# Entry of a fused adaLN transformer block: c turned on the tensor engine, modulation weights by tile, q and k side by side, high parts by ScalarE

## The chip, the cores and the metric

One core of a Trainium2 chip runs the whole program. The metric is the device time of one execution in microseconds (us). The engines are named as in the profile: PE is the tensor engine (PEld its weight loads), DVE the vector engine, ACT the scalar engine (ScalarE), POOL GpSimd, SP the queue that issues most transfers. Each engine works through its own instructions in order and waits on semaphores for the others.

## What is computed

The block is adaptive layer norm, attention with 32 heads, and a gated feed-forward part, on 2048 rows of 576 values. Only the front of it matters here:

```
mod = (silu(c) @ w_mod)            # c: 1 x 576, w_mod: 576 x 3456, six vectors of 576
h   = layernorm(x) * (1 + ca) + sa # x: 2048 x 576; sa, ca are the first two of the six
q, k, v = h @ wqkv                 # then softmax attention, projection, feed-forward
```

Products are made in 32-bit accuracy: an operand is split into a rounded "high" part (type fp32r) and a "low" part, the rest, and three products (high x high, high x low, low x high) are added up in PSUM.

## The kernel before

**Constants of c.** `craw` (128 x 5) takes c with its 576 values spread over the partitions (L403, L404), ACT makes the sigmoid (L405) and loads the table of the exponential ahead (L407), DVE multiplies (L408) and spreads the result over 32 columns each into `mrow` (L424), where `modulate` takes it as PE's weights.

**Modulation.** `load_mod` loads the first third of w_mod, 576 x 1152, into `wm`: two transfers of two row tiles of 128 and one of the last 64 rows (L124, L125). `modulate` (L149) multiplies them into one PSUM bank: for row tiles 0 to 4 a 384- and a 192-column product for each of two vectors, then, once more over all five tiles, the 64 columns that are left. DVE copies the result to `row`, PE transposes it (L190), and DVE writes the two vectors as columns `mcol` (L200, L201).

**Rows.** x comes in four chunks of 512 rows (4 tiles each, `rows_in`). `normalized` makes statistics on DVE (L207, L208), the inverse root with one power on POOL (L221) and eight small DVE steps, and scales the four x tiles (L232). PE transposes them with an identity matrix (`ident`, L241). `ln_transpose` (L244) then works in five steps over the 576 features: ACT applies `mcol` and writes `full` in fp32 (L251), DVE rounds it to the high part in `hT` (L259) and subtracts for the low part (L260); the fifth step is half as high and has its high and low part both on DVE (L264 to L266).

**Queries, keys, values.** `project_qk` takes one weight tile for q and one for k through 14 products of 512 columns each (L336) into one PSUM bank each; ACT takes the high part (L342), DVE the low part (L343), and SP stores both. `project_v` does the same for 288 columns of v (L389, L394) into `vaug`, which POOL fills with ones first (L458). `splits` and `split_v` make the high part of the weights on ACT (L277) and the low part on DVE (L278).

**Order.** In this entry the three engines PE, DVE and ACT run exactly in the order in which the code is written (a manual schedule); a scheduler places POOL and SP work. Chunk by chunk the code reads: q/k products, v products, transposes and modulation of the next chunk, statistics of the chunk after it. After the entry a second stage makes the other q/k tiles (the list `tiles`) while scores of the first heads are already multiplied for their maxima: `project_qk` there calls `run`, which issues four score products (L550) after each accumulation; DVE reduces each (L556). Seven PSUM banks go round in the order of allocation for all of these, so which score waits for which earlier bank follows from that order. Here the scheduler sets the order.

Of the kernel before, what the change touches and what calls it, by code (L numbers as in the profile page):

```python
# [15 lines left out]
F32 = mybir.dt.float32  # L16
# [7 lines left out]
P = 128  # L24
S = 2048
D = 576
# [59 lines left out]
def tile_block(ctx, tc, x_in, wqkv, wo, w_gate, w_up, w_down, c_in, w_mod, out):  # L86
# [62 lines left out]
    def modulate(row, wm, pieces, takes, between=()):  # L149
# [8 lines left out]
        pm = bank()  # L158
        for parts in pieces:
            for t in range(last + 1):  # L160
                if between and t == 2 and parts is pieces[0]:
                    between[0]()
                k = ksize(t)
                for v in range(2):
                    for g, to, f0, n in parts:
                        q = 32 * (2 * v + g)
                        nc.tensor.matmul(
                            pm[q : q + 32, to : to + n], sc_b[:k, t, :],
                            wm[t][:k, v * D + f0 : v * D + f0 + n],
                            start=t == 0, stop=t == last, tile_position=(0, q),  # L170
                        )
        if between:
            between[1]()
        if pieces is HALVES:
# [12 lines left out]
        if between:  # L187
            between[2]()
        for b in range(3):
            nc.tensor.transpose(pt[:, b * P : (b + 1) * P], row[:, b * P : (b + 1) * P], ident)  # L190
        cols = pt[:, 0:384].rearrange("p (b q) -> p b q", q=P)
        for v, (dst, add) in enumerate(takes):
# [51 lines left out]
    def ln_transpose(pool, zs, dst, c0, turned=()):  # L244

        cols = slice(c0, c0 + 512)
        for i in range(5):
# [79 lines left out]

    def project_qk(both, ahead=None):

        pl = stages[0].tile([P, 2, 1024], F32R, name="pl")  # L330
        for i, ((parts, wh, wl), ch) in enumerate(both):
            acc = bank()
            cols = slice(ch * 512, (ch + 1) * 512)
            ts_ = terms(wh, wl, slice(0, P))
            for n, (w, t) in enumerate(ts_):
                nc.tensor.matmul(  # L336
                    acc, w, hT[:, t, cols], start=n == 0, stop=n == len(ts_) - 1
                )
            if ahead:
# [60 lines left out]
    with tc.tile_pool(name="ln", bufs=2) as ln:  # L400
        craw = early.tile([P, 5], F32, name="craw")
        nc.vector.memset(craw, 0.0)
# [3 lines left out]
        warm = early.tile([P, 1], F32, name="warm")  # L406
        nc.scalar.activation(warm, sc[:, 0:1], AF.Exp)  # L407
        nc.vector.tensor_mul(sc, sc, craw)  # L408

        def rows_in(ch):  # L410
# [7 lines left out]
        def normalized(xs, first=None):  # L418
            mv = ln.tile([P, 4, 2], F32, name="mv")
            rs = ln.tile([P, 4], F32, name="rs")  # L420
            for j, xt in enumerate(xs):
                ln_stats(ln, xt[:, :D], mv[:, j, :])
            if first is not None:
                nc.vector.tensor_copy(  # L424
                    first[:, 384:544].rearrange("p (t c) -> p t c", c=32), sc.unsqueeze(2).to_broadcast([P, 5, 32])
                )
# [10 lines left out]
        wvp = wv0.enter_context(tc.tile_pool(name="wv0", bufs=1))  # L437
        with tc.tile_pool(name="wmp", bufs=1, side="right") as wmp:
            rows_now = rows_in(0)
            wm = wmp.tile([P, 5, 2 * D], F32, name="wm")  # L440
            wm = load_mod(wm[:, 0:4, :], wm[:, 4, :], 0)
            row = wmp.tile([P, 544], F32, name="mrow")
            zs = normalized(rows_now, row)
# [8 lines left out]
            for _ in modulate(  # L452
                row, wm, QUARTERS, [(mcol[:, 1, :], 0.0), (mcol[:, 0, :], 1.0)],
                (turn_some(0, 1, 2), turn_some(3), turn_some(4)),
            ):
                pass
        stages.append(right.enter_context(tc.tile_pool(name="stage", bufs=2, side="right")))
        nc.gpsimd.memset(vaug, 1.0)  # L458
        splits[0]()
        ln_transpose(ln, None, hT, 0, turned)  # L460
        splits[1]()
        split_v()
        with tc.tile_pool(name="kdp", bufs=1) as kdp:
            zs = normalized(rows_now)
            pls = []
            for ch in range(NCH):
                pls.append(project_qk([(wt, ch) for wt in wts]))
                project_v(wv, 0, 4 * ch)
# [1370 lines left out]
```

## Time and profile before

| what | value |
|---|---|
| median of 3 runs (lowest, highest) | 2770.05 us (2768.8, 2773.7) |
| the profiled execution, its own time | 2771.59 us |
| its span in the profile | 2769.8 us |
| PE busy, share of the span | 99% |
| DVE busy | 83% |
| ACT busy | 57% |
| POOL busy | 30% |
| granted TensorE clock, mean | 0.999 of full |

The span is what the profile covers; the execution's own time lies 1.8 us above it. The page divides the span into 40 slices of 69 us, and PE is busy 90% or more in all but the first (70%). So the entry is the stage where PE has most of its idle time, and the rows further down are taken from the first 80 us, and from the stage of the score maxima around 145 us.

### The profile page before, as it was taken

The numbers are of one execution on the slowest core, as the hardware profiler recorded it, in microseconds if no ns is written. First come the engines' busy times: TensorE is split into PE (matmuls) and PEld (weight loads), VectorE is DVE, ScalarE is ACT, GpSimd is POOL, SyncE is SP. The second block draws the span as 40 slices with busy tenths as digits, with TensorE's granted clock in tenths as the row PEclk, the third lists the DMA queues.
The fourth block names the chain that finished last, engine by engine and source line by source line (L and its number), as shares of the span: only waits on it lengthen the run. The fifth ranks groups of instructions, "written<-read, shape, count | busy, mean of one in ns | idle before, by whom it ended". The sixth has DMA issues, their size and how long they took to land.

```text
span 2769.8 us, 50752 instructions
## 1 busy us (share of the span) xinstructions
PE 2735.4 (99%) x18429; PEld 1829.0 (66%) x18429; DVE 2291.4 (83%) x4333; ACT 1590.3 (57%) x3020; POOL 838.6 (30%) x1061
## 2 busy tenths in 40 slices
PE   7999999999999999999999999999999999999999
PEld 5975444444444544444444888888888888888888
DVE  7278989999999889999883888888888677777777
ACT  3215999999999789999987323333333122222221
POOL 3122237888853214660133222222221100000000
PEclk9999999999999999999999999999999999999999
DMA  5342344555553121332246766767768965656653
GB/s 175 122 153 98 89 106 170 189 189 188 185 174 104 51 64 55 137 98 74 64 115 240 250 225 230 243 221 268 278 239 295 330 203 195 203 196 201 199 198 117
DMA packets 185378, 480.03 MB, mean 173 GB/s; under 512 B 30304, under 2 KB 94308, under 8 KB 175016
## 3 DMA queue, kind: packets, MB, share of 16 engines
q1 hardware_dynamic: 164216, 377.39, 41.0%
q0 software_dynamic: 20912, 99.41, 10.0%
q8 instruction: 145, 2.38, 0.4%
q14 instruction: 105, 0.86, 0.1%
HBM read 294.80 MB, written 181.38 MB: 172 GB/s over the span
## 4 chain that ended last, share of the span: by engine, by line
PE 92%; DVE 3%; DMA 2%; POOL 1%; issue 1%; SPq 0%; ACT 0%; DVEq 0%; ACTq 0%; POOLq 0%
PE x L1226 27%; PE o L655 19%; PE s L1070 12%; PE s L550 10%; PE d L1376 8%; PE d L1308 6%; PE s L336 4%; PE s L799 2%; PE s L389 1%; DMA big<-in_w_mod_dram 1%; POOL big L141 0%; PE d L1574 0%; DVE Oa L1380 0%; DVE w L1216 0%; DMA raw<-in_B_w_up_dram 0%
## 5 line engine op out<-in xcount | busy, mean ns | idle before, releaser
L1074 ACT ACTIVATE p<-s 128x512 f32<-128x512 f32 x2048 | 1069.9, 626 | 85.4 <-PE s L1070 60.2
L556 DVE TENSOR_REDUCE mx<-s 128x1 f32<-128x512 f32 x1568 | 1001.3, 684 | 102.8 <-PE s L550 72.1
L655 PE MATMUL o<-p,vaug 128*32 128x256 f32 (+1 forms) x5848 | 594.8, 477 | 2.0 <-ACT oT L673 2.0
L550 PE MATMUL s<-k,q 54*128 54x512 f32 x1920 | 550.2, 436 | 0.0
L1070 PE MATMUL s<-q,k 56*128 56x512 f32 x1920 | 530.8, 439 | 1.3 <-DMA q<-mrows 1.3
L1070 PEld LDWEIGHTS s<-q,k 56*128 56x128 f32 x1920 | 251.8, 185 | 252.8 <-DVE mx L556 74.2
L550 PEld LDWEIGHTS s<-k,q 54*128 54x128 f32 x1920 | 277.8, 185 | 210.6 <-DVE mx L561 65.3
L1226 PE MATMUL x<-k,w 128*128 128x512 f32 x1512 | 368.1, 391 | 0.0
L1226 PEld LDWEIGHTS x<-k,w 128*128 128x128 f32 x1512 | 277.3, 188 | 53.4 <-issue 1.7
L655 PEld LDWEIGHTS o<-p,vaug 128*32 128x32 f32 x5848 | 117.1, 108 | 205.6 <-issue 188.0
L1226 PE MATMUL x<-big,w 128*128 128x512 f32 x1008 | 246.1, 393 | 4.9 <-DVE u L1740 4.9
L1376 PE MATMUL d<-wd,hh 128*128 128x288 f32 x1248 | 249.6, 295 | 0.9 <-DMA wd<-wds 0.5
L1226 PE MATMUL x<-w,w 128*128 128x512 f32 x1008 | 244.6, 391 | 0.0
L1226 PEld LDWEIGHTS x<-big,w 128*128 128x128 f32 x1008 | 186.6, 189 | 41.0 <-DVE u L1740 5.3
L1226 PEld LDWEIGHTS x<-w,w 128*128 128x128 f32 x1008 | 184.5, 188 | 33.9
L1376 PEld LDWEIGHTS d<-wd,hh 128*128 128x128 f32 x1248 | 202.3, 188 | 4.4 <-DMA wd<-wds 0.9
L1376 PE MATMUL d<-wd,hl 128*128 128x288 f32 x624 | 184.5, 296 | 0.0
L1380 DVE TENSOR_TENSOR Oa<-Oa,d 128x288 f32<-128x288 f32 x312 | 136.7, 453 | 54.9 <-PE d L1376 50.9
L561 DVE CUSTOM_DVE_ANT_0 over<-s,over 128x512 f32<-128x512 f32 x240 | 163.8, 682 | 0.9
L559 ACT ACTIVATE over<-s 128x512 f32<-128x512 f32 x240 | 147.9, 616 | 3.0 <-PE s L550 1.0
L1235 ACT ACTIVATE sg<-x 128x512 f32<-128x512 f32 x36 | 21.5, 598 | 206.8 <-PE x L1226 206.7
L1207 ACT CAST w<-S 128x768 fp32r<-128x768 f32 x71 | 59.4, 836 | 137.3 <-POOL S L1180 135.4
(265 smaller groups left out, 3820.4 us busy)
## 6 DMA issues: line engine op xcount, KB each, us to landing
ws<-w SPq DMA_DIRECT2D x126, 640.0 KB
w<-ws SPq DMA_DIRECT2D x126, 640.0 KB
wd<-wds SPq DMA_DIRECT2D x19, 1152.0 KB
k<-kd SPq DMA_DIRECT2D x60, 360.0 KB
wds<-w POOLq DMA_DIRECT2D x18, 1152.0 KB, 5.2
wtd<-t POOLq DMA_DIRECT2D x32, 576.0 KB, 4.8
wt<-wtd SPq DMA_DIRECT2D x64, 288.0 KB
wd<-wds SPq DMA_DIRECT2D x52, 288.0 KB
```

Of the source, the lines that this page charges most:

```text
L336: nc.tensor.matmul(acc, w, hT[:, t, cols], start=n == 0, stop=n == len(ts_) - 1)
L550: nc.tensor.matmul(sp, qs[rows, qt * P : (qt + 1) * P], ks[rows, at * 512 : (at + 1) * 512], start=True, stop=True,)
L556: nc.vector.tensor_reduce(to, sp, axis=AX.X, op=ALU.max)
L559: nc.scalar.activation(over, sp, AF.Relu)
L561: nc.vector.tensor_tensor_reduce(out=over, in0=sp, in1=over, scale=1.0, scalar=LOWEST, op0=ALU.add, op1=ALU.max, accum_out=mx[:, h * n + q ...
L655: nc.tensor.matmul(acc[32 * j : 32 * j + 32, cols], vaug[:, kt, (2 * p + h) * VW : (2 * p + h) * VW + 32], probs[2 * c + h][:, cols], star ...
L1070: nc.tensor.matmul(sT, ks[rows, kcols], qs[rows, c * 512 : (c + 1) * 512], start=True, stop=True)
L1074: state["exp"] = nc.scalar.activation(pr, sT, AF.Exp, scale=SCALE)
L1226: nc.tensor.matmul(acc[v], w[:, v, a, :], X[s][:, b, :], start=first and n == 0, stop=n == 6, skip_group_check=not first,)
L1308: nc.tensor.matmul(acc, a[:, rows], w[:, k, :], start=n == 0, stop=n == 2)
L1376: nc.tensor.matmul(acc[:, :HALF], a[:, f, rows], w[:, f, cols], start=n == 0, stop=n == 5)
L1380: nc.vector.tensor_add(Oa[:, t, cols], Oa[:, t, cols], acc[:, :HALF])
```

## The change

c is loaded as five rows of 128 on ACT's queue into the scratch tile `row`, multiplied by its sigmoid there, and turned to columns by one PE transpose, placed between the third and the fourth x tile's statistics. `load_mod` has one transfer for each row tile when it is called for the first third. `modulate` goes over the row tiles once and puts the last 64 columns into a second PSUM tile of the pool `po`; the transposes of x that stood among its products now stand behind them. `ln_transpose` has ACT write the high part too, straight from PSUM, in place of DVE's rounding. `project_qk` allocates both banks at its start, and for chunk 0 alternates between q and k in groups of three products. Both weight splits stand ahead of chunk 0's modulation. POOL's fill of `vaug` becomes 17 small ones that write only the columns of ones.

```
     def load_mod(a, b, i):
         cols = slice(2 * D * i, 2 * D * (i + 1))
+        if not i:
+            for t in range(5):
+                k = ksize(t)
+                nc.sync.dma_start((a[:, t, :] if t < 4 else b)[:k], w_mod[t * P : t * P + k, cols])
+            return [a[:, t, :] for t in range(4)] + [b]
...
         pm = bank()
-        for parts in pieces:
-            for t in range(last + 1):
-                if between and t == 2 and parts is pieces[0]:
-                    between[0]()
+        pms = [pm] if pieces is HALVES else [pm, po.tile([P, 512], F32, name="o")]
+        for t in range(last + 1):
+            for to_, parts in zip(pms, pieces):
...
-            nc.vector.tensor_copy(row[:, 0:256], pm[:, 0:256])
+            nc.vector.tensor_copy(row[:, 0:192], pm[:, 0:192])
             for q in (0, 64):
-                nc.vector.tensor_copy(row[q : q + 32, 256:384], pm[q : q + 32, 256:384])
+                nc.vector.tensor_copy(row[q : q + 32, 192:384], pm[q : q + 32, 192:384])
+                q += 32
+                nc.vector.tensor_copy(row[q : q + 32, 192:256], pms[1][q : q + 32, 192:256])
...
             if i < 4:
                 modulated(full, 0, P)
-                nc.vector.tensor_copy(dst[:, i, cols], full)
+                modulated(dst[:, i, cols], 0, P)
                 nc.vector.tensor_sub(dst[:, 4 + i, cols], full, dst[:, i, cols].bitcast(F32))
...
-    def project_qk(both, ahead=None):
+    def project_qk(both, ahead=None, together=False):
+        accs = [bank() for _ in both]
+        all_ = [terms(wh, wl, slice(0, P)) for (_, wh, wl), _ in both]
+        places = [(i, n) for i in range(len(both)) for n in range(len(all_[i]))]
+        if together:
+            places.sort(key=lambda at: min(at[1] // 3, 4))
+        for i, n in places:
...
-        nc.sync.dma_start(craw[:, 0:4], c_in[0, 0:DM].rearrange("(t p) -> p t", p=P))
-        nc.sync.dma_start(craw[0:64, 4:5], c_in[0, DM:D].rearrange("(p o) -> p o", o=1))
-        nc.scalar.activation(sc, craw, AF.Sigmoid)
...
+                if first is not None and j == 3:
+                    turned_c = po.tile([P, 512], F32, name="o")[:, 0:5]
+                    nc.vector.tensor_mul(first[0:5, 256:384], first[0:5, 0:P], first[0:5, P:256])
+                    nc.tensor.transpose(turned_c, first[0:5, 256:384], ident[0:5, 0:5])
...
+            nc.scalar.dma_start(row[0:4, 0:P], c_in[0, 0:DM].rearrange("(t p) -> t p", p=P))
+            nc.scalar.dma_start(row[4:5, 0:64], c_in[0:1, DM:D])
...
-        nc.gpsimd.memset(vaug, 1.0)
-        splits[0]()
+        ones = vaug[:, :, 0 : H * VW].rearrange("p t (h e) -> p t h e", e=VW)
+        for t in range(NT):
+            nc.gpsimd.memset(ones[:, t, :, DH:VW], 1.0)
+        nc.gpsimd.memset(vaug[:, :, H * VW :], 1.0)
+        for split in splits:
+            split()
         ln_transpose(ln, None, hT, 0, turned)
-        splits[1]()
         split_v()
```

What that does to the order on the engines is seen at three places. On SP, the first place is the head of the program, here before and then with the change:

```order
L414 DMA x<-in_A_x_dram 128x576
L403 DMA craw<-in_c_dram 128x4x1
L404 DMA craw<-in_c_dram 64x1
L414 DMA x<-in_A_x_dram 128x576 x3
L124 DMA wm<-in_w_mod_dram 128x2x1152 x2
L125 DMA wm<-in_w_mod_dram 64x1152
L270 DMA wq_raw<-in_A_wqkv_dram 128x4x128
```

```order
L417 DMA x<-in_A_x_dram 128x576 x4
L125 DMA wm<-in_w_mod_dram 128x1152 x4
L125 DMA wm<-in_w_mod_dram 64x1152
L276 DMA wq_raw<-in_A_wqkv_dram 128x4x128
L280 DMA wq_raw<-in_A_wqkv_dram 64x128 x2
```

The two transfers of c are gone from between the first and the second x tile, and w_mod comes in five pieces in place of three.

On ACT, the second place is chunk 0, from the weights' high part on, before and then with the change (`full` and `hT` are what the modulation writes, `s_...` the transposed x in PSUM):

```order
L277 CAST wq_h<-wq_raw 128x640
L251 ACTIVATE full<-s_234,mcol 128x512
L251 ACTIVATE full<-s_239,mcol 128x512
L251 ACTIVATE full<-s_244,mcol 128x512
L251 ACTIVATE full<-s_271,mcol 128x512
L251 ACTIVATE full<-s_281,mcol 128x512
L277 CAST wq_h<-wq_raw 128x640
L277 CAST wv_h<-wv_raw 128x1440
```

```order
L283 CAST wq_h<-wq_raw 128x640 x2
L257 ACTIVATE full<-s_261,mcol 128x512
L257 ACTIVATE hT<-s_261,mcol 128x512
L257 ACTIVATE full<-s_266,mcol 128x512
L257 ACTIVATE hT<-s_266,mcol 128x512
L257 ACTIVATE full<-s_271,mcol 128x512
L257 ACTIVATE hT<-s_271,mcol 128x512
L257 ACTIVATE full<-s_286,mcol 128x512
L257 ACTIVATE hT<-s_286,mcol 128x512
L257 ACTIVATE full<-s_291,mcol 128x512
L283 CAST wv_h<-wv_raw 128x1440
```

Each chunk has nine activations in place of five, and both weight casts now stand ahead of the first. The other three chunks read alike.

On PE, the third place is the stage of the score maxima, with bank numbers (`s5_1441` is a tile in bank 5; `hT` products are a q/k accumulation, `t1,q0` products are scores), with the change only; before, four scores always stood together behind an accumulation:

```order
L344 MATMUL s5_1441<-hT_123,wq_l_1436 128x512
L567 MATMUL s3_1484<-t1_1058,q0_1050 128x512
L567 MATMUL s4_1487<-t1_1058,q0_1050 128x512
L567 MATMUL s6_1493<-t1_1058,q0_1050 128x512
L344 MATMUL s0_1510<-hT_123,wq_h_1435 128x512 x2
L344 MATMUL s0_1510<-hT_123,wq_l_1436 128x512
L567 MATMUL s5_1490<-t1_1058,q0_1050 128x512
L344 MATMUL s0_1510<-hT_123,wq_l_1436 128x512
L344 MATMUL s0_1510<-hT_123,wq_h_1435 128x512
```

With both banks taken at the start of `project_qk`, the third score of the second group falls on the bank that the accumulation just finished (5). The scheduler has put it behind the first 11 products of the next accumulation (the pair of rows above it stands for a run of 11), and DVE's low part of that bank ahead of its fourth reduction. This occurs 11 times. Further on, the engines' orders are the same as before, but for one exchange of two loads on SP ahead of this stage.

## Rows read from the trace of the kernel before

**Rows 1.** Page: busy time, share of the span, instructions of each engine.

```profile
PE 2735.4 (99%) x18429; PEld 1829.0 (66%) x18429; DVE 2291.4 (83%) x4333; ACT 1590.3 (57%) x3020; POOL 838.6 (30%) x1061
```

**Rows 2.** PE's waits, 0 to 110 us: total us, times, longest.

```profile
PE s L167 <- DMA wm<-in_w_mod_dram: 12.2, 1, 12.2
```

**Rows 3.** Timeline to 24 us: start, us, engine, line, operation [idle before, releaser].

```profile
1.19 0.42 SPq L403 DMA_DIRECT2D craw<-in_c_dram  x1
...
2.29 1.52 SPq L414 DMA_DIRECT2D x<-in_A_x_dram  x3
...
8.73 0.27 DVE L424 COPY mrow<-sc 128x160 f32<-128x160 f32 x1
...
17.86 0.16 PEld L167 LDWEIGHTS s<-wm,mrow 64*32 64x32 f32 x8 [0.62 <-DMA wm<-in_w_mod_dram]
...
18.97 0.73 ACT L277 CAST wq_h<-wq_raw 128x640 fp32r<-128x640 f32 x1 [10.74 <-DMA wq_raw<-in_A_wqkv_dram]
...
19.55 0.42 DVE L182 COPY mrow<-s 128x256 f32<-128x256 f32 x1 [5.09 <-PE s L167]
...
21.29 2.85 ACT L251 ACTIVATE full<-s,mcol 128x512 f32<-128x512 f32 x4 [1.59 <-DVE mcol L201]
```

**Rows 4.** Stretches: span, length, PE busy (count), clock, DMA share, GB/s.

```profile
1.50:4.00 2.50, 0.00 (x0) 1.00 0.66 135
4.00:13.00 9.00, 0.77 (x10) 1.00 0.97 349
```

**Rows 5.** Timeline of chunks 0 and 1, 22 to 47 us.

```profile
22.56 0.69 DVE L260 TENSOR_TENSOR hT<-full,hT 128x512 fp32r<-128x512 f32 x1
...
23.17 0.42 DVE L259 CAST hT<-full 128x512 fp32r<-128x512 f32 x1
...
28.70 1.65 DVE L278 TENSOR_TENSOR wv_l<-wv_raw,wv_h 128x1440 fp32r<-128x1440 f32 x1
...
30.27 0.81 DVE L207 BATCH_NORM_STATS2 st<-x 128x6 f32<-128x288 f32 x2
...
37.03 2.05 DVE L232 TENSOR_SCALAR x<-x,mv,rs 128x576 f32<-128x576 f32 x4
...
39.21 2.65 PE L241 MATMUL s<-ident,x 128*128 128x128 f32 x20
...
39.91 2.86 ACT L251 ACTIVATE full<-s,mcol 128x512 f32<-128x512 f32 x4
...
46.59 0.82 DVE L207 BATCH_NORM_STATS2 st<-x 128x6 f32<-128x288 f32 x2
```

**Rows 6.** Timeline of chunk 2 and the start of chunk 3, 56 to 77 us.

```profile
56.96 2.12 ACT L251 ACTIVATE full<-s,mcol 128x512 f32<-128x512 f32 x3 [2.30 <-PE s L241]
...
57.76 1.29 POOL L364 TENSOR_TENSOR kd_e<-pl 128x512 f32<-128x512 f32 x1 [0.91 <-DVE pl L343]
57.77 1.55 DVE L259 CAST hT<-full 128x512 fp32r<-128x512 f32 x1
...
59.36 1.67 DVE L260 TENSOR_TENSOR hT<-full,hT 128x512 fp32r<-128x512 f32 x1
...
67.13 0.82 DVE L207 BATCH_NORM_STATS2 st<-x 128x6 f32<-128x288 f32 x2
...
76.11 2.08 PE L241 MATMUL s<-ident,x 128*128 128x128 f32 x17 [0.17 <-DVE x L232]
```

**Rows 7.** A stretch behind it, PE: span, length, PE busy (count), clock, DMA share, GB/s.

```profile
90.00:110.00 20.00, 20.00 (x113) 1.00 0.68 213
```

**Rows 8.** Timeline in the stage of the score maxima, one period.

```profile
145.41 0.73 PE L550 MATMUL s<-t,q 54*128 54x512 f32 x4
145.94 2.48 DVE L556 TENSOR_REDUCE mx<-s 128x1 f32<-128x512 f32 x4 [0.98 <-PE s L550]
...
148.34 0.68 DVE L343 TENSOR_TENSOR pl<-s,pl 128x512 fp32r<-128x512 f32 x1
149.47 0.73 PE L550 MATMUL s<-t,q 54*128 54x512 f32 x4
```

More of the change, by code (lines that the diff above doesn't have):

```diff
@@ L172, in modulate @@
         if between:
-            between[1]()
+            between[0]()
         if pieces is HALVES:
@@ L181, in modulate @@
             nc.vector.memset(row[:, 256:384], 0.0)
-            nc.vector.tensor_copy(row[:, 0:256], pm[:, 0:256])
+            nc.vector.tensor_copy(row[:, 0:192], pm[:, 0:192])
             for q in (0, 64):
-                nc.vector.tensor_copy(row[q : q + 32, 256:384], pm[q : q + 32, 256:384])
+                nc.vector.tensor_copy(row[q : q + 32, 192:384], pm[q : q + 32, 192:384])
+                q += 32
+                nc.vector.tensor_copy(row[q : q + 32, 192:256], pms[1][q : q + 32, 192:256])
         yield
         pt = bank()
-        if between:
-            between[2]()
         for b in range(3):
             nc.tensor.transpose(pt[:, b * P : (b + 1) * P], row[:, b * P : (b + 1) * P], ident)
+        if between:
+            between[1]()
         cols = pt[:, 0:384].rearrange("p (b q) -> p b q", q=P)
@@ L326, in load_qk @@
         return parts, wh, wl
-    def project_qk(both, ahead=None):
+    def project_qk(both, ahead=None, together=False):
         pl = stages[0].tile([P, 2, 1024], F32R, name="pl")
[L331 to L338, printed above, removed]
+        accs = [bank() for _ in both]
[4 more added lines that the diff above has]
+        for i, n in places:
+            (w, t), ch = all_[i][n], both[i][1]
+            nc.tensor.matmul(
+                accs[i], w, hT[:, t, ch * 512 : (ch + 1) * 512],
+                start=n == 0, stop=n == len(all_[i]) - 1, skip_group_check=together,
+            )
+            if n < len(all_[i]) - 1:
+                continue
+            acc = accs[i]
             if ahead:
@@ L400, in tile_block @@
     with tc.tile_pool(name="ln", bufs=2) as ln:
-        craw = early.tile([P, 5], F32, name="craw")
-        nc.vector.memset(craw, 0.0)
-        nc.sync.dma_start(craw[:, 0:4], c_in[0, 0:DM].rearrange("(t p) -> p t", p=P))
-        nc.sync.dma_start(craw[0:64, 4:5], c_in[0, DM:D].rearrange("(p o) -> p o", o=1))
-        nc.scalar.activation(sc, craw, AF.Sigmoid)
-        warm = early.tile([P, 1], F32, name="warm")
-        nc.scalar.activation(warm, sc[:, 0:1], AF.Exp)
-        nc.vector.tensor_mul(sc, sc, craw)
         def rows_in(ch):
@@ L421, in normalized @@
             for j, xt in enumerate(xs):
+                if first is not None and j == 3:
+                    turned_c = po.tile([P, 512], F32, name="o")[:, 0:5]
+                    nc.vector.tensor_mul(first[0:5, 256:384], first[0:5, 0:P], first[0:5, P:256])
+                    nc.tensor.transpose(turned_c, first[0:5, 256:384], ident[0:5, 0:5])
                 ln_stats(ln, xt[:, :D], mv[:, j, :])
             if first is not None:
+                nc.vector.tensor_copy(sc, turned_c)
                 nc.vector.tensor_copy(
@@ L438, in tile_block @@
         with tc.tile_pool(name="wmp", bufs=1, side="right") as wmp:
+            row = wmp.tile([P, 544], F32, name="mrow")
+            nc.vector.memset(row[0:5, 0:P], 0.0)
+            nc.scalar.dma_start(row[0:4, 0:P], c_in[0, 0:DM].rearrange("(t p) -> t p", p=P))
+            nc.scalar.dma_start(row[4:5, 0:64], c_in[0:1, DM:D])
             rows_now = rows_in(0)
+            nc.scalar.activation(row[0:5, P:256], row[0:5, 0:P], AF.Sigmoid)
+            warm = early.tile([P, 1], F32, name="warm")
+            nc.scalar.activation(warm[0:5], row[0:5, P : P + 1], AF.Exp)
             wm = wmp.tile([P, 5, 2 * D], F32, name="wm")
             wm = load_mod(wm[:, 0:4, :], wm[:, 4, :], 0)
-            row = wmp.tile([P, 544], F32, name="mrow")
             zs = normalized(rows_now, row)
@@ L453, in tile_block @@
                 row, wm, QUARTERS, [(mcol[:, 1, :], 0.0), (mcol[:, 0, :], 1.0)],
-                (turn_some(0, 1, 2), turn_some(3), turn_some(4)),
+                (turn_some(0, 1, 2), turn_some(3, 4)),
             ):
@@ L466, in tile_block @@
             for ch in range(NCH):
-                pls.append(project_qk([(wt, ch) for wt in wts]))
+                pls.append(project_qk([(wt, ch) for wt in wts], together=not ch))
                 project_v(wv, 0, 4 * ch)
```

2 lines of the change are left out of this document (1 added, 1 removed).

## Prediction

> **What bounds the kernel now.** I read the page first: PE is busy for 99% of the span [rows 1], so a gain can only come from where PE stands still. PE's waits say where: the largest is one wait of 12.2 us for the first modulation weights, at the start [rows 2]. Then I followed the first 80 us in the timeline to see how long the entry holds PE back. From the transposes of chunk 3, which start at 76.11, PE no longer pauses: 20.00 us busy of 20 from 90 to 110 [rows 6, 7]. Everything behind that keeps its order on every engine but for the maxima stage, so a us won or lost before 76.11 arrives at the end, and one won on an engine that PE doesn't wait for is lost.
>
> The 76 us fall into two parts. Up to 21.29, when ACT modulates the first tile, transfers set the time: the last weight tile lands at 17.86 (W), PE, DVE copies and PE's transposes of the two vectors follow, and ACT starts 3.43 later (F) [rows 3]. From there to 76.11 the path is on DVE: PE takes the low parts as they come, and the next chunk's statistics stand behind them in DVE's order (at 30.27, 46.59, 67.13), their scaling ahead of the next transposes [rows 5, 6].
>
> **Transfers (the first term).** Before, c's two transfers stand between the first x tile and the rest: the issue of c starts at 1.19 and that of the next x tile at 2.29, so 1.10 us of SP [rows 3]. c also comes as 576 single values, and from 1.5 to 4 the engines move 135 GB/s at a share of 0.66, against 349 GB/s at 0.97 from 4 to 13 [rows 4]. Had the first stretch run at the second's rate, 2.5 x 214 GB/s = 0.54 MB more would have been moved, worth 1.5 us. Bounds for the earlier arrival of all that is behind c: 1.1 (only SP's time) and 1.5; I take 1.3, so W' = 16.6. The same 2.65 MB of weights now come in five transfers; PE starts on the first earlier, but the last tile alone sets W'. c's own path doesn't count: before, its columns were ready at 9.0 (8.73 + 0.27), far ahead of W [rows 3]; it would have to be 7 us later to matter. `ident`, which c's transpose needs, no longer waits behind POOL's long fill of ones.
>
> **From W to F.** Eight of the ten 64-column products no longer stand behind the last tile, while 12 transposes of x now do: at 2.65 us for 20 [rows 5] they are 1.6 us of PE. They run while DVE copies the row (0.42 for the first copy before [rows 3], five copies now in place of three), so their cover is about as long as they are. I keep 3.4 us, with +0.6 and -0.5 as bounds: F' = 20.0. A second gate is ACT's own order: both weight casts of 0.73 now stand ahead of the first modulation. The first started at 18.97 when its weights landed [rows 3]; 1.3 earlier is 17.7, two casts end at 19.1, under the 20.0. Were the second weight tile to land 1.6 later than the first, the cover would be gone. DVE's second weight split, also put ahead, runs while ACT does its first two activations.
>
> **High parts on ACT (the second term).** DVE loses a rounding of 0.42 in each of four steps, ACT gets one more activation of 2.85 / 4 = 0.71 [rows 3, 5]. A chunk's ACT work grows to nine activations, so DVE's low parts now follow ACT, one each 1.42 us. Before, a cast and a subtraction took about 1.1 a step. Start of the first activation to start of the next thing in DVE's order, after: eight activations 5.70, the ninth to its end about 0.8, two half-high roundings of 0.45 and the last subtraction to its successor 0.62, with 0.06 of handover = 8.0. By chunks:
>
> - Chunk 0: then the low part of v's weights, 28.70 to 30.27 = 1.57 [rows 5]: 9.6 to the statistics of chunk 1. Before 30.27 - 21.29 = 8.98. Loss 0.6.
> - Chunk 1: before 46.59 - 39.91 = 6.68 [rows 5], now 8.0, loss 1.3. Something is won back ahead of it: the scaling of x ended at 39.08 (37.03 + 2.05), but PE was with v until 39.21 and ACT started at 39.91, 0.83 later. Alternating q and k lets PE end chunk 0 soon after the last low part; it then stands ready, has turned three of four tiles, and ACT starts about 0.35 behind the scaling. Net loss 0.8.
> - Chunk 2: before 67.13 - 56.96 = 10.17 [rows 6], far more than chunk 1's 6.68, because POOL makes the key differences: while its operation of 1.29 ran, a rounding took 1.55 in place of 0.42 and a subtraction 1.67 in place of 0.69 [rows 5, 6]. Without the roundings DVE has room: two or three subtractions are still held up by about 1 us, but each may take 1.42. Now 8.0 to 8.7, gain 1.5 to 2.2; I take 1.8.
> - Chunk 3: from the scaling on PE has v products to do while ACT works. ACT's last high part is later than DVE's was by about 1.3, and those products cover it barely; without cover it costs up to 0.5.
>
> The sum from F to 76.11 is 0.6 + 0.8 - 1.8 = -0.4. Bounds: -0.9 (no collision left) and +1.5 (collisions as before, chunk 3 uncovered).
>
> On chunk 2's collision the Trainium skill (SBUF — State Buffer, "SBUF: two separate sides") says that DVE and GpSimd share one port pair as an exclusive lock, against a DVE copy in its fast mode or one with two SBUF inputs, and that ScalarE never waits there. By that rule the roundings' share of the loss is gone and the subtractions' stays, which is the middle of my range for chunk 2; the trace agrees (1.55 and 1.67 beside 0.42 and 0.69).
>
> **Maxima stage (the third term).** The third score of every second group has to wait until DVE has emptied bank 5, 11 times. A period is 18 products in 149.47 - 145.41 = 4.06, 0.2256 each [rows 8]. The score stands 3 + 11 products behind the group's first: 14 x 0.2256 = 3.16, at 148.57 in this period. DVE starts at 145.94, makes three reductions of 0.60 and the low part of 0.68: bank free at 148.42. That is 0.15 in hand, so no cost; 0 to +1 as the bound (0.1 late, 11 times). The 16 small fills of `vaug` on POOL, the PSUM tile from `po` and the second store order lie beside all this: 0.
>
> **Sum.** -1.3 - 0.4 + 0 = -1.7, taken from the profiled execution's own 2771.6: 2769.9. That execution lies 1.5 above the median of the three runs (2770.05), so as a median: 2768.3. A difference of 0.2%, 5.5 us, is about what a measurement of this kernel tells from none (its three runs span 4.9); so the likeliest outcome is a small gain that counts as no change.
>
> **The rivals.**
>
> - Weights land no sooner. Five transfers mean more that complete one behind the other, and the small pieces of q/k weights still mix with the last tile. Then F' = 21.0 at best: -0.3 - 0.4 = about -0.7, 2769.4 as a median. For it: the last 64 rows landed only at 17.86 though they were issued right behind the rest. Against it: the engines were full from 4 to 13 [rows 4], so bytes ahead count. Chance 0.17.
> - ScalarE becomes the bound. If chunk 2's subtractions stay as slow as before and chunk 3 isn't covered, the second term is +1.5 or, with the collisions added to ACT's pace, +2.8: -1.3 + 2.8 = +1.5, 2771.6. For it: 1.42 a step against 1.1. Against it: nothing holds DVE in chunks 0, 1 and 3 now. Chance 0.10. The Trainium skill (ScalarE: Activation LUTs, "Rules for kernel authors") advises the vector engine for simple elementwise work for being faster; by that rule this edit alone is a loss, and the trace agrees on the single operation (0.71 against 0.42).
> - More is gained: w_mod's tiles land at full rate, ACT is gated only by the q/k weights (18.4), -2.9 - 0.9 = -3.8: 2766.3. For it: PE waits 12.2 us there in all. To pass 5.5 it needs another us that I don't see. Chance 0.17, of which 0.06 beyond 5.5.
> - Slower: the maxima stage. If DVE runs one reduction (0.60) and 0.2 more behind, the bank is 0.66 late, 11 times = 7.3, minus the 1.7 won: +5.6, 2775.6. It decides from a delay of 0.8 in DVE against the 0.15 in hand. For it: the margin is small, and DVE is busy 3.2 of 4.06 us. Against it: the four reductions start 0.53 behind PE in this period, with idle time before them. Chance 0.06.
>
> **How the numbers follow.** The forecast has 0.50, the rivals 0.17, 0.10, 0.17 and 0.06. Its own range is -1.5 - 0.9 - 0.5 to -1.1 + 1.0 + 0.6, that is 2767.2 to 2770.6; with 1.5 of scatter of a median on either side and the gain rival below, 2765.0 to 2771.8 holds all but the slower case and the far end of the gain: 8 in 10. Faster by over 0.2%: 0.06. Slower: 0.06. Within: 0.88.
>
> **What would show it.** The last weight tile's products at about 16.6 and ACT's first modulation near 20.0; pairs of activations without gaps, the statistics of chunks 1 and 2 later against F by 0.6 and 1.4, those of chunk 3 earlier by 0.4; chunk 3's transposes near 74.4; no wait of PE for DVE at the scores around 140 to 235. It would be wrong if the q/k weights gate ACT beyond 20, if the v weights land behind ACT's ninth activation, or if scores wait.

## The result, and the profile after

The changed kernel takes 2779.77 us (median of 20 runs, 2773.15 to 2784.42); the kernel before, in 20 runs beside it, 2772.46. The ratio is 1.0028, 95% interval 1.0022 to 1.0034: 7.3 us slower (6.1 to 9.4). The forecast was 2768.3 and its range ended at 2771.8.

First the page of after. PE is busy for 99% of the span as before [rows 1], but with 7.7 us more of it:

```profile
PE 2743.1 (99%) x18430; PEld 1829.7 (66%) x18430; DVE 2286.3 (82%) x4320; ACT 1600.6 (58%) x3036; POOL 832.1 (30%) x1077
```

The entry did what was forecast, and more. Timeline of after: start, us, engine, line, operation:

```profile
15.77 0.83 PE L171 MATMUL s<-wm,mrow 64*32 64x384 f32 x7 [0.56 <-DMA wm<-in_w_mod_dram]
...
16.55 1.53 PE L247 MATMUL s<-ident,x 128*128 128x128 f32 x12
...
19.20 0.78 ACT L257 ACTIVATE full<-s,mcol 128x512 f32<-128x512 f32 x1 [0.40 <-DVE mcol L207]
...
28.55 0.81 DVE L213 BATCH_NORM_STATS2 st<-x 128x6 f32<-128x288 f32 x2
45.57 0.82 DVE L213 BATCH_NORM_STATS2 st<-x 128x6 f32<-128x288 f32 x2
64.68 0.82 DVE L213 BATCH_NORM_STATS2 st<-x 128x6 f32<-128x288 f32 x2
72.28 0.73 PE L247 MATMUL s<-ident,x 128*128 128x128 f32 x2
```

The last weight tile's products start at 15.77 (W) against 17.86 [rows 3], ACT's first modulation at 19.20 (F) against 21.29. From there the first scores of the maxima stage follow at 138.96; before, they stood at 141.35. So 2.4 us were won, in this execution. The issue of the modulation weights starts at 2.60 in place of 3.85, and from 1.5 to 4 the DMA engines move 267 GB/s in place of 135 [rows 4]; the row of after, with the columns of rows 4:

```profile
1.50:4.00 2.50, 0.00 (x0) 1.00 0.87 267
```

Then the stage of the maxima, from its first score to the first score behind its last product, in one row for each kernel: stretch, length, busy time (instructions) of PE, PEld, DVE, ACT and POOL, granted clock, DMA share, GB/s. Before:

```profile
141.35:234.47 93.12, 93.12 (x412) 65.60 (x411) 71.92 (x117) 16.23 (x28) 26.03 (x25) 1.00 0.48 160
```

After:

```profile
138.96:239.66 100.70, 100.70 (x413) 66.67 (x412) 72.97 (x117) 16.23 (x28) 25.96 (x25) 1.00 0.45 148
```

The same products and scores at the same clock take 7.58 us longer, and PE has no idle time in either row. A PE that is 100% busy hides this: a loss inside it shows only in the count and the length side by side. One period of after, PE's rows, shows the place:

```profile
142.71 0.39 PE L344 MATMUL s<-hT,wq_l 128*128 128x512 f32 x1
143.03 0.73 PE L567 MATMUL s<-t,q 54*128 54x512 f32 x3
143.69 0.74 PE L344 MATMUL s<-hT,wq_h 128*128 128x512 f32 x2
...
145.89 0.63 PE L344 MATMUL s<-hT,wq_h 128*128 128x512 f32 x2
146.45 0.50 PE L567 MATMUL s<-t,q 54*128 54x512 f32 x1
146.88 0.50 PE L344 MATMUL s<-hT,wq_l 128*128 128x512 f32 x1
147.22 0.40 PE L344 MATMUL s<-hT,wq_h 128*128 128x512 f32 x1
147.46 0.39 PE L344 MATMUL s<-hT,wq_l 128*128 128x512 f32 x1
147.78 0.73 PE L567 MATMUL s<-t,q 54*128 54x512 f32 x4
```

Three scores take 0.66 to the next product (143.03 to 143.69), as four do in rows 8. The third score, now alone at 146.45, sits 0.56 behind the start of a pair of products that would have passed in 0.46, and the next product starts only 0.43 behind it. From group to group it is 4.75 in place of 4.06 [rows 8]: 0.69, eleven times.

### The profile page after: what moved, and what is told of

It reads as the page before. It is cut to its first block, busy times and chain, and to the rows that moved or that the text cites. A ratio compares the mean times of both kernels' runs of the same rounds, so it can differ in the third digit from the quotient of the medians.

```text
span 2771.4 us, 50777 instructions
## 1 busy us (share of the span) xinstructions
PE 2743.1 (99%) x18430; PEld 1829.7 (66%) x18430; DVE 2286.3 (82%) x4320; ACT 1600.6 (58%) x3036; POOL 832.1 (30%) x1077
## 3 DMA queue, kind: packets, MB, share of 16 engines
q0 software_dynamic: 20912, 99.41, 10.1%
q8 instruction: 145, 2.38, 0.4%
## 4 chain that ended last, share of the span: by engine, by line
PE 95%; DVE 2%; DMA 1%; issue 1%; ACT 0%; POOL 0%; SPq 0%; DVEq 0%; ACTq 0%; POOLq 0%
PE x L1243 28%; PE o L672 20%; PE s L1087 13%; PE s L567 11%; PE d L1393 8%; PE d L1325 6%; PE s L344 4%; PE s L816 2%; PE s L401 1%; DMA wq_raw<-in_A_wqkv_dram 0%; DMA raw<-in_B_w_up_dram 0%; PE d L1591 0%; DVE Oa L1397 0%; DVE w L1233 0%; PE s L927 0%
```

## The experiments

W (start of the last weight tile's products), F (ACT's first modulation), the first score and the stage (as in the rows above) are read from each kernel's profile; medians and ratios stand against runs of the kernel before on the same chip. All kernels from "groups of 1 and 3" on have banks late.

| kernel | median (runs) | before | ratio, 95% interval | W | F | first score | stage |
|---|---|---|---|---|---|---|---|
| changed | 2779.77 (20) | 2772.46 | 1.0028, 1.0022 to 1.0034 | 15.77 | 19.20 | 138.96 | 100.70 |
| changed, again | 2779.74 (1) | 2773.34 | | 15.99 | 21.30 | 141.06 | 100.70 |
| banks late | 2772.63 (11) | 2772.16 | 1.0001, 0.9992 to 1.0009 | 16.56 | 21.23 | 140.95 | 93.26 |
| before, banks early | 2779.25 (10) | 2772.16 | 1.0026, 1.0017 to 1.0036 | 18.74 | 22.17 | 142.20 | 100.24 |
| groups of 1 and 3 | 2785.21 (4) | 2772.16 | 1.0050, 1.0036 to 1.0063 | 16.03 | 21.35 | 140.44 | 107.52 |
| heads apart | 2782.32 (4) | 2772.16 | 1.0035, 1.0022 to 1.0048 | 15.82 | 21.14 | 140.91 | 103.38 |
| groups of 2 and 2 | 2782.68 (4) | 2773.34 | 1.0035, 1.0022 to 1.0049 | 15.81 | 21.13 | 140.22 | 103.40 |
| high parts by DVE | 2774.52 (10) | 2773.02 | 1.0002, 0.9993 to 1.0010 | 15.52 | 20.84 | 140.46 | 93.26 |
| one tile behind | 2771.89 (10) | 2773.02 | 0.9995, 0.9987 to 1.0004 | 15.80 | 20.13 | 139.92 | 93.26 |
| busy start | 2773.47 (11) | 2773.02 | 0.9999, 0.9991 to 1.0008 | 15.80 | 20.48 | 140.25 | 93.25 |
| busy start, one tile | 2772.94 (12) | 2773.02 | 1.0001, 0.9993 to 1.0010 | 15.03 | 18.45 | 138.26 | 93.26 |
| busy throughout, mixed | 2774.51 (11) | 2773.34 | 1.0001, 0.9991 to 1.0010 | 16.38 | 19.80 | 137.97 | 93.25 |
| mixed | 2769.70 (11) | 2773.34 | 0.9987, 0.9977 to 0.9997 | 15.90 | 19.87 | 138.08 | 93.26 |

From the end of the stage to the end of the span, where no edit reaches, the profiles take from 2531.7 us (changed) to 2546.3 (busy start, one tile); before's takes 2535.3. So one profile gives the stage well (93.25 or 93.26 with banks late and whole groups), but not the total.

### The maxima stage

**Banks late.** The changed kernel, with the order of banks of before:

```
-        accs = [bank() for _ in both]
+        accs = [bank() for _ in both] if together else []
...
             (w, t), ch = all_[i][n], both[i][1]
+            if len(accs) <= i:
+                accs.append(bank())
```

> The changed kernel, but project_qk takes the second bank only when the first accumulation is done, as before, except in the one call that takes q and k in turns. The third score of a second group then no longer falls on the bank just accumulated, and all groups have four scores again. Theory (a score that stands alone costs PE time: no partner to pass beside, and two more turns from products to a score and back; 0.69 x 11 = 7.6): the period is 4.06 again and the stage ends 7.6 earlier than in the changed kernel, so the new entry's 2.4 is all that is left: profile 2769.2 against 2771.6 of before. Rival (the score waits for DVE to empty its bank): the same, since the wait goes too. Second question, the granted clock: if the lower clock of most runs of the changed kernel (0.996 to 0.998, against 0.999 of the profiled one) comes with the maxima stage, the median is some 2.4 under before's (ratio 0.9991); if it comes with the new entry, the median stays some 4 above what the profile says (ratio 1.0005 to 1.001).

The stage is 93.26 again and the median is back at that of before. What is not there is the entry's gain: F stood at 21.23 in this profile, so the first score came at 140.95, 0.4 earlier than before. As for the mean clock, the kernel before has runs from 0.995 to 0.999 too beside these: it is no mark of the change, and the second question started from a wrong premise.

**Banks early**, the counterpart on the kernel before:

```
+        accs = [bank() for _ in both]
         for i, ((parts, wh, wl), ch) in enumerate(both):
-            acc = bank()
+            acc = accs[i]
```

> The kernel before, with one edit: project_qk takes both banks at its start. The lone scores appear, the entry stays as it was. Theory and rival alike: the period of two groups grows from 4.06 to 4.75 eleven times, 7.6 us, profile 2779 (or some 2 to 3 less, if waits further on that were open before are filled). If the lower clock comes with the maxima stage, the median is another 3 to 5 above that (ratio 1.004 to 1.005); if with the entry, the ratio is 1.002 to 1.0027.

7.1 us longer in stage and median. This line alone makes the result.

**Groups of 1 and 3**, on the kernel with banks late (`ahead` now takes the number of scores):

```
+            if ahead and n == 10:
+                ahead(1)
             if n < len(all_[i]) - 1:
                 continue
             acc = accs[i]
             if ahead:
-                ahead()
+                ahead(3)
```

> As the first of these runs (banks as before), but each group of four scores is cut in one and three by hand: one score behind product 11 of each accumulation, three at its end. The banks rotate as before, so each score finds a bank that has been free for long. Theory (a lone score costs an own slot of 0.23 and two more switches of together 0.46): each of the 22 groups costs 0.69 more, 15.2 us over the first run. Rival (it was the wait for DVE's release of the bank): no bank is late, so the time of the first run, at most 1 us more.

Its PE rows, with a period of 4.71:

```profile
151.18 0.73 PE L571 MATMUL s<-t,q 54*128 54x512 f32 x3
...
154.02 0.61 PE L346 MATMUL s<-hT,wq_h 128*128 128x512 f32 x2
154.56 0.49 PE L571 MATMUL s<-t,q 54*128 54x512 f32 x1
154.98 0.50 PE L346 MATMUL s<-hT,wq_l 128*128 128x512 f32 x1
...
155.89 0.73 PE L571 MATMUL s<-t,q 54*128 54x512 f32 x3
```

The stage is 14.26 longer than with banks late; its first score stands three products earlier (0.69), so 13.6 or 0.62 a group. The lone score has the same gaps around it, 0.54 and 0.42, though the banks come free as in the kernel before, early enough for whole groups. The wait for DVE is not the cause. In the changed kernel, too, each of the 11 lone scores starts 0.40 or 0.41 behind the end of DVE's low part.

**Heads apart**, on the kernel with banks late. The four scores of a group all belong to one head, in place of two in turns:

```
-                h, kc = state.get("at") or MAXIMA[i % 8]
+                h, kc = state.get("at") or (sorted(MAXIMA) if turns["s"] <= 64 + 4 * LEAD else MAXIMA)[i % 8]
```

> As the first of these runs, but the order of the scores in this stage is changed so that the four of a group are all of one head (all on the same half of PE's rows) in place of the two heads in turns. No score stands alone and no switch is added. Theory, its part about partners (scores of the two heads pass side by side, so four cost two slots of 0.23): two more slots in each of 22 groups, 0.46 x 22 = 10 us over the first run, a group of four takes 1.1 in place of 0.66. If partners don't matter and the lone score's price is all in the switches: no change.

PE's rows of one group:

```profile
149.99 1.20 PE L569 MATMUL s<-t,q 54*128 54x512 f32 x4
151.12 0.74 PE L346 MATMUL s<-hT,wq_h 128*128 128x512 f32 x2
```

1.13 to the next product in place of 0.66, and the stage is 10.1 longer (103.38): 0.46 in each of 22 groups, two slots of 0.23. Scores of the two heads, which lie on the two halves of PE's rows, pass side by side; scores of one head pass one behind the other.

**Groups of 2 and 2**, as 1 and 3, but with `ahead(2)` at both places.

> New entry and banks late, each group of four scores cut by hand in two and two: one pair behind product 11 of each accumulation, one pair at its end. All pairs stay pairs, so no slot is added; only the turns from products to scores and back are doubled. Theory (a cut into one and three costs 0.64 a group, of which a slot is 0.23, so the turns are 0.41): the stage from the first score to the last product is 22 x 0.41 = 9.0 longer than 92.9. Rival (all of the price is the missing partner): 92.9, no change.

Its PE rows around a pair inside an accumulation:

```profile
148.66 0.63 PE L346 MATMUL s<-hT,wq_h 128*128 128x512 f32 x2
149.22 0.51 PE L571 MATMUL s<-t,q 54*128 54x512 f32 x2
149.65 0.50 PE L346 MATMUL s<-hT,wq_l 128*128 128x512 f32 x1
149.99 0.40 PE L346 MATMUL s<-hT,wq_h 128*128 128x512 f32 x1
```

The stage is 10.14 longer, 9.45 without the three products: 0.43 a group with no pair broken. So a turn from products to scores and back costs 0.43 and the missing partner 0.23, together 0.66 against the 0.69 measured in the changed kernel. The turn costs about as much at the end of an accumulation (0.4, from the period of before), so it isn't the place inside an accumulation that makes the price. The Trainium skill (TensorEngine Tiling (Array Packing), "Key Properties") says that changing the tiling mode drains the tensor engine. The trace agrees in that the score instructions use 54 of the rows, the products all 128, and each way back and forth costs what this run shows; no run separates a drain from whatever else may cost time in a turn.

### The entry

**The changed kernel again**, for a second profile.

> The changed kernel itself once more, for a second profile of it: three of the profiles with the same entry showed PE at half clock when the last weight tile landed and 4.7 to 5.3 from there to the first modulation, its own one showed full clock and 3.4. Theory (its own profile was a lucky one, as its time of 2773.2 was the lowest of 20): first modulation near 21.2, first scores near 140.9, the maxima stage 100.4 long, end 2 to 6 later than in the first profile. Rival (the entry of the changed kernel differs from that of the other runs): first modulation at 19.2 again.

PE and ACT in its timeline:

```profile
15.99 1.49 PE L171 MATMUL s<-wm,mrow 64*32 64x384 f32 x7
...
17.42 2.82 PE L247 MATMUL s<-ident,x 128*128 128x128 f32 x12
20.03 0.85 PE L194 MATMUL s<-ident,mrow 128*128 128x128 f32 x3
...
21.30 0.78 ACT L257 ACTIVATE full<-s,mcol 128x512 f32<-128x512 f32 x1 [2.58 <-DVE mcol L207]
```

The weights land as early as in the first profile, but the 12 transposes take 2.82 in place of 1.53 and the products 1.49 in place of 0.83: W to F is 5.31 in place of 3.43, and the entry's gain is down to 0.3. 0.3 won and 7.6 lost agrees with the 7.3 of the medians; the first profile, of the fastest of 20 runs, was the exception. In eight profiles with this order of transposes W to F was 3.43 once and 4.67 to 5.32 seven times; with the old order 3.43 both times. But the old order pays for slow transposes too, ahead of W. In the profile of banks early, whose entry is that of before, they take 2.77 in place of 1.55, PE is busy for all of the 6.83 us from 11.91 to W, and its weight load there waits for no transfer:

```profile
14.62 2.77 PE L241 MATMUL s<-ident,x 128*128 128x128 f32 x12
...
18.74 0.15 PEld L167 LDWEIGHTS s<-wm,mrow 64*32 64x32 f32 x8 [0.62 <-issue]
```

So W, F and the first score are 0.9 later there than in before's own profile. Against that profile (142.20) the changed kernel's second one is 1.1 ahead: how much the entry wins depends on which profiles are set side by side. That the slow transposes come from PE's clock is seen in the profile of the run with one tile behind, from W to F: 0.50 of full, the lower level of 1.2 GHz (columns as above):

```profile
15.80:20.10 4.30, 3.82 (x22) 2.59 (x23) 1.77 (x10) 1.45 (x2) 0.00 (x0) 0.50 1.04 308
```

**One tile behind** the last products, in place of three, on the kernel with banks late:

```
-                (turn_some(0, 1, 2), turn_some(3, 4)),
+                (turn_some(0), turn_some(1, 2, 3, 4)),
```

> The first run of the study with one edit: only one of the five tiles of x (4 transposes in place of 12) is turned between the last products and the row's transposes, the other four behind them. Theory (at half clock the 12 transposes, 2.8, outlast the five copies of the row, 1.5, which they were to lie beside): where the profile falls at half clock, the first modulation starts about 0.9 earlier than at 21.2 (20.3); at full clock nothing changes (19.1 to 19.2, since the copies then set it). Rival (the copies or the landing set it): no change at either clock. In the median at most 1 us.

At half clock W to F is 4.33, 1.0 less. The interval of its ratio doesn't tell it from before.

**Busy start**, on the kernel with banks late. PE transposes the identity 24 times from 1.6 on and 8 times behind c, into a bank that nobody reads; the first of the two places:

```
+        busy = ps[0].tile([P, 512], F32, name="s0")
+        for _ in range(24):
+            nc.tensor.transpose(busy[:, 0:P], ident, ident)
```

> The first run of the study (new entry, banks late) with one addition: PE, which has nothing to do before the first weight tile lands at about 9, transposes the identity 24 times from 1.6 on and 8 times more behind c's transpose, into a bank that nobody reads. No result changes. Theory (the new entry gives its 2 us back because PE still runs at half clock when the last weight tile lands, so that products, 12 transposes of x and the row's transposes take 4.7 to 5.3 from landing to the first modulation in place of 3.4): with PE busy from the start the products of the first tile already take 0.83 for seven in place of 1.48, the 12 transposes 1.5 in place of 2.8, and ACT starts its first modulation 3.4 behind the last landing, at 19.2 to 20.0 in place of 21.1 to 21.4. Median 1.5 to 2.5 under the first run's, ratio to before 0.9992 to 0.9995. Rival (the long way from landing to modulation comes from the landing order of weights, or from DVE's copies): the way stays 4.7 to 5.3, no change.

Half of it came true. The first tile's products ran at full speed, but between tiles PE waited again (1.61 and 0.85 ahead of the last two), and at the last tile it was at half clock once more:

```profile
8.87 0.81 PE L171 MATMUL s<-wm,mrow 128*32 128x384 f32 x7 [0.25 <-DVE var L226]
...
14.11 0.83 PE L171 MATMUL s<-wm,mrow 128*32 128x384 f32 x7 [1.61 <-DMA wm<-in_w_mod_dram]
...
15.80 1.35 PE L171 MATMUL s<-wm,mrow 64*32 64x384 f32 x7 [0.85 <-DMA wm<-in_w_mod_dram]
...
17.10 2.62 PE L247 MATMUL s<-ident,x 128*128 128x128 f32 x12
```

The granted clock of the same run, in stretches:

```profile
13.00:16.10 3.10, 1.15 (x18) 0.66 (x22) 0.88 (x3) 0.00 (x0) 1.04 (x3) 0.98 1.15 188
16.10:19.50 3.40, 3.40 (x24) 2.70 (x17) 1.41 (x5) 1.45 (x2) 0.00 (x0) 0.52 1.08 339
```

PE was busy 1.15 of 3.1 us, and behind that the clock was at 0.52. The median did not move (0.9999).

**Both together** (busy start, one tile behind):

> Both edits at once: PE busy from 1.6 on, and one tile of x behind the last products. Theory: first modulation at 19.1 to 19.9 in every run, the way from the last landing 3.3; median 1.5 to 2.5 under the first run's and the lowest so far, ratio to before 0.9990 to 0.9995. Rival (the entry's gain is lost further on, whatever the first modulation does): median as the first run's, ratio 1.000.

In this profile the clock stayed up, although PE waited as in the last one (1.61 and 0.77 ahead of the last two tiles): W to F 3.42, first score 138.26, 3.1 earlier than before. So such waits don't always lower the clock. The median didn't follow (1.0001), and this profile has the longest rest behind the stage.

**High parts by DVE**, on the kernel with banks late:

```
-                modulated(dst[:, i, cols], 0, P)
+                nc.vector.tensor_copy(dst[:, i, cols], full)
```

> The first run of the study with the high parts of x rounded by DVE again, as before (one activation and one rounding a step in place of two activations). The prediction's second term says that ScalarE's high parts win 0.4 from the first modulation to the transposes of chunk 3 (chunk 0 +0.6, chunk 1 +0.8, chunk 2 -1.8): so this run is 0.4 later there, its statistics of chunks 1 and 2 earlier, of chunk 3 later. Rival (ScalarE is the slower engine for it, and the collision with GpSimd in chunk 2 stays): this run is 1 to 1.5 earlier there. In the median within 0.05% of the first run.

From F to the statistics of chunks 1, 2, 3 and to chunk 3's transposes it takes 8.80, 24.76, 45.36 and 52.96; in the changed kernel 9.35, 26.37, 45.48 and 53.08; before 8.98, 25.30, 45.84 and 53.44. So ScalarE loses 0.55 in chunk 0 and 1.06 in chunk 1 and wins 1.49 in chunk 2. Taken by itself the edit is worth nothing (0.12 later at the transposes); the small gain over before comes from the rest of the change.

**Mixed.** That run says where each engine is better. With one tile behind and banks late:

```
-                modulated(dst[:, i, cols], 0, P)
+                if c0 < 1024:
+                    nc.vector.tensor_copy(dst[:, i, cols], full)
+                else:
+                    modulated(dst[:, i, cols], 0, P)
```

> The version that the runs so far point to: new entry, banks late, one tile of x behind the last products, and high parts rounded by DVE in chunks 0 and 1 and by ScalarE in chunks 2 and 3. Theory (from the two profiles that differ only in who rounds: DVE is 0.55 faster in chunk 0 and 1.06 in chunk 1, ScalarE 1.5 in chunk 2): from the first modulation to the transposes of chunk 3 it takes 51.5 in place of 53.1; the first modulation stands at 20.1 at half clock, 19.1 at full; the median is 1.6 under that of the run with one tile behind, some 2 to 3 under before, ratio 0.9989 to 0.9993. Rival (the collision with GpSimd's key differences moves to another chunk when DVE gets there earlier): 53 as before, ratio 0.9995.

Its F, the three statistics and chunk 3's transposes:

```profile
19.87 2.11 ACT L257 ACTIVATE full<-s,mcol 128x512 f32<-128x512 f32 x3 [0.97 <-DVE mcol L207]
...
28.66 0.81 DVE L213 BATCH_NORM_STATS2 st<-x 128x6 f32<-128x288 f32 x2
44.65 0.82 DVE L213 BATCH_NORM_STATS2 st<-x 128x6 f32<-128x288 f32 x2
63.77 0.82 DVE L213 BATCH_NORM_STATS2 st<-x 128x6 f32<-128x288 f32 x2
71.36 0.73 PE L247 MATMUL s<-ident,x 128*128 128x128 f32 x2
```

F to the transposes is 51.49, as worked out, and the first score stands 3.3 earlier than before. It is the only version whose interval lies below before: ratio 0.9987 (0.9977 to 0.9997). Seven versions without the lone scores were measured, so one such interval can be chance, and the two others with first scores 3.1 and 3.4 earlier show no gain. That this version is faster is suggested, not shown.

**Busy throughout, mixed.** The version just named, with the busy start and 4, 10 and 4 more transposes of the identity ahead of the third, fourth and fifth tile's products:

```
+            if between and t > 1:
+                for _ in range((4, 10, 4)[t - 2]):
+                    nc.tensor.transpose(busy[:, 0:P], ident, ident)
```

> The version just named, with PE kept busy from 1.6 on and also between the weight tiles: 4, 10 and 4 transposes of the identity ahead of the third, fourth and fifth tile's products, where PE waited 0.6, 1.6 and 0.8. Theory (the clock of the run with a busy start fell again because PE waited for tiles): PE is at full clock when the last tile lands, 12 profiles of 12; from the last landing to the first modulation 3.4, not 4.3 to 5.3; first scores of the maxima stage at 137 against 141.4; ratio 0.9984 to 0.9988. Rival (how busy PE was doesn't set the clock there): the way from landing to modulation is above 4 and the ratio that of the run without the busy work. A second way to fail: where the transposes run at half clock, ten of them hold up the fourth tile's products by 0.7.

PE kept its clock: W to F is 3.42. It also did with busy start and one tile behind alone, so it isn't shown that the added transposes are needed. But W was 16.38, so F was 19.80 and the first score 137.97, no better than without the busy work, and the median is 4.8 higher than that of the mixed version. Its profile loses time at a place behind the entry; PE's row there, then the stretches around it:

```profile
807.11 0.59 PE L1100 MATMUL s<-q,k 56*128 56x512 f32 x1 [2.38 <-DMA q<-mrows]
```

```profile
800.00:804.00 4.00, 4.00 (x40) 1.55 (x36) 3.81 (x7) 3.84 (x8) 1.27 (x1) 1.00 0.98 303
804.00:807.60 3.60, 1.23 (x10) 0.64 (x6) 1.46 (x4) 1.28 (x3) 0.00 (x0) 0.96 0.40 137
807.60:811.00 3.40, 3.40 (x24) 1.04 (x21) 1.84 (x3) 2.07 (x4) 0.60 (x1) 0.50 0.37 100
811.00:814.40 3.40, 3.40 (x18) 1.03 (x14) 2.04 (x5) 2.82 (x6) 0.00 (x0) 0.54 0.70 208
```

PE waits 2.38 for a transfer of row maxima and then runs 6.8 us at 0.52 of full clock, which by estimate loses 6.8 x 0.48 = 3.3 more: 5.7 in all. In before the wait at this place is 0.93, and the clock from 800 to 816 stays at 1.00. But this place doesn't explain the median: the profile of the mixed version takes even longer behind the stage (2540.9 against 2539.1). Why the two busy versions gain nothing stays open.

## Why the prediction was wrong

**The maxima stage** is the step that failed: "A period is 18 products in 149.47 - 145.41 = 4.06, 0.2256 each", and from it "That is 0.15 in hand, so no cost". The 18 were taken as equal. They are 14 products at 0.229 (3.21) and four scores, which pass in two slots (the 0.23 of one product) and cost 0.4 for the turn there and back. The question asked was only whether a bank is late. It isn't: in after DVE's low part ends at 146.04, and the score starts at 146.45, 0.33 behind the start of the last product (145.89 + 0.23), as it is in whole groups (142.71 to 143.03 above, 0.32). The price was in taking the score out of its group: 0.69 x 11 = 7.6. The rival "Slower: the maxima stage" named the place, and got 0.06 for a delay of DVE that never came. That its 0.66 for each of the 11 lies near the 0.69 measured is luck. "No wait of PE for DVE at the scores" was right, and no sign of safety.

**Transfers**: right in kind (267 GB/s in place of 135 from 1.5 to 4), undersized in ten of twelve profiles. W is 1.3 to 2.8 earlier than 17.86 in the profiles of the new entry (15.03 to 16.56), 2.09 in the first one, against a bound of 1.5. The prediction took 17.86 for the landing alone. But in before PE is busy for all of the 5.63 us from its first products (12.23) to there, so W could fall to the landing of the last tile only because PE now starts on the first one at 9.14. No run separates c's transfers from the five pieces.

**From W to F**: "I keep 3.4 us, with +0.6 and -0.5 as bounds" failed in most runs. The 12 transposes were priced from one row at full clock; at half clock they take 2.82, longer than the five copies of the row that were to cover them (17.63 to 19.08 in the second profile). Half clock costs 1.9 from W to F, of which 1.0 goes away with one tile behind; it eats what the transfers won. The second gate held: both weight casts end at 18.80 in the first profile, ahead of F.

**High parts**: right, also chunk by chunk against F: +0.37 (forecast 0.6), +0.70 (0.8), -1.43 (-1.8), sum -0.36 (-0.4). Of the sum, ScalarE itself makes +0.12 (the prediction's +0.6, +1.3 and -1.8 make +0.1) and the other edits -0.48 (the prediction's -0.5 for q and k in turns); no run separates these. On chunk 2 the Trainium skill (SBUF — State Buffer, "SBUF: two separate sides") lets ScalarE pass while DVE and GpSimd hold each other up; the trace agrees, with 1.49 between the two ways of rounding. The subtractions stayed slow, but there is nearly room for that: in after they take 1.10 to 1.61 each in chunk 2 against 0.69 in chunk 0, and ACT needs 1.33 for a pair of activations. Durations in ns (min/median/max), first and last start, chunk 0 and chunk 2:

```profile
L266 DVE TENSOR_TENSOR hT<-full,hT x4: 691/692/693, 20.7 to 24.7; 128x512 fp32r<-128x512 f32 x4
L266 DVE TENSOR_TENSOR hT<-full,hT x4: 1096/1387/1612, 57.4 to 61.4; 128x512 fp32r<-128x512 f32 x4
```

Chunk 3 was covered: from its transposes to the first score 66.68 against 66.62. These start at 74.73 in before; the 76.11 that the prediction took for their start is that of the last 17 of 20, whose counterpart in after stands at 73.66 (forecast 74.4).

**Sum**: forecast -1.7; measured -2.4 + 7.6 in the first profile, -0.3 + 7.6 in the second. The first profile's own time is even so only 1.6 above that of before's (2773.15 against 2771.59), since it was 3.6 shorter behind the stage, which no edit here explains.

**Range**: before's median was 2772.46 in the 20 runs beside the change, 2.4 above the three that the sum started from and above the end of the range: without the loss in the maxima stage, the change (banks late, 2772.63) would still have come out beyond 2771.8. Its upper end also adds only +1.0 where two terms had upper bounds, +1.5 (high parts) and +1 (maxima stage).

## What to carry to other kernels

When an order listing shows an instruction pulled out of a group, price the group with it and without it before asking what it waits for: small matmuls that pass in pairs lose their partner and pay one more turn there and back, and PE's idle time shows none of it. Work moved from in front of a late transfer to behind it needs a price at both clock levels, since a PE that is left waiting there can fall to the lower one (it did in one of two profiles with the same waits). One profile of a changed kernel can be its best run: compare its time with the median before reading a gain from it.

## What the runs showed of the hardware

- Going from 128-row products to 54-row scores and back costs PE 0.43 us here, with no idle time in the profile; two scores on different row halves share a slot of 0.23.
- At the start of the program the clock column shows 1.00 in stretches where matmuls take twice their time (the second profile of the changed kernel, whose transposes from 17.42 on take 0.235 each in place of 0.13). There the duration of a known instruction is the better clock. Its row:

```profile
16.00:19.00 3.00, 3.00 (x22) 2.15 (x21) 1.33 (x5) 1.45 (x2) 0.00 (x0) 1.00 0.91 263
```

- A wait of PE can be paid twice: 2.38 for a transfer, then by estimate 3.3 for the half clock behind it (busy throughout, mixed); at 0.93 in the same place, in before, the clock stayed up. Time goes with the mean granted clock for one and the same kernel: of 77 runs of the kernel before beside the experiments, the 17 at 0.999 have a median of 2770.1, the 22 at 0.996 one of 2775.5. This is the scatter against which effects of 1 us can't be told.
